# Chunked attention and two feed-forward layers: weighted sum and next scores as one stretch, side work at other times

## The chip, the cores and the metric

The kernel runs on one core of a Trainium2 chip. Times are device microseconds (us) of one execution. Three runs of the kernel before took 1117.49, 1117.62 and 1117.96 us; their median, 1117.62 us, is what the changed kernel is compared with. TensorE is called PE here, its weight loads PEld, VectorE DVE, ScalarE ACT, GpSimd POOL and SyncE, which issues nearly all DMAs, SP.

## The reference

Inputs are float32: q, k, v of 4 batches, 8 heads, 768 positions, 64 values a head; 8 memory keys and values a head; five weight matrices.

```
chunk, left_ctx, right_ctx = (32, 16, 8)           # n_mem = 8
for c in range(nc):                                # 24 chunks
    k_full = concat([mem_k, k[l_start:r_end]])     # 8 + up to 56 keys
    scores = q_c @ k_full.T / 8
    a = exp(scores - max); a = a / (sum(a) + 1e-09)
    out[c] = a @ v_full
x = out as 3072 tokens x 512
h = relu(x @ w_in);  x = (h * h) @ w_out           # 512 -> 2048 -> 512
g = x @ w_gate; silu = g / (1 + exp(-g))
y = (silu * (x @ w_val)) @ w_out2                  # 512 -> 1536 -> 512
```

## The kernel before

**Attention in units.** The 3072 queries are 24 units of 128 queries, all 8 heads each. A unit (class `Unit`) loads q, k and v (L522), and then goes through five steps: `scores` (A: 16 small float32 matmuls, 32 in the trace, into one PSUM bank), `weigh` (B: maximum, subtraction, exponential, sum, reciprocal and scaling, on DVE, ACT and in part POOL), `turn` (T: 16 DVE transposes of 32x32 blocks, L617, or for the first units `turn_pe`, four PE transposes, L639), `mix` (M: the weighted sum of v, 16 small float32 matmuls, L668) and `leave` (L: the result is split in a high and a low part). Units 0 to 3 come first of all, 4 to 7 beside the first quarter of the first feed-forward layer (j = 0), 8 to 23 beside j = 1, 2, 3. The table `BESIDE` says at which step i of which j each letter of a unit is put into the program.

**Feed-forward layers.** All other matmuls work on pairs of fp32r parts, three products for one (`TERMS`). In the first layer four blocks of 512 tokens are done directly: `first_layer` (L843, 12 matmuls) and `first_out` (L870, four times 3 matmuls). For the last two blocks and for the whole second layer, a 2x2 block product is done in seven products: `quads` (L1099) and `out_layer` (L1236). These need sums and differences of weight blocks, the "left sides" (`sides`, `Left`): loaded from DRAM, added on DVE or POOL, split (L467 on ACT, L474 on DVE or POOL), written back to DRAM and loaded again as the weights of the products. The second layer's 18 sides come from the weights in DRAM (`words`), the 16 of the first layer from the parts that j = 1 and 2 wrote back (`whole_of`, L1040). Sums of the data, the "right sides" (`rights`), are made the same way, L486 and L474.

**What sets the order.** The code only lists operations with their buffers and a cost per engine. `Plan.run` then plays them through in its own time and writes the instructions of every engine in the order found. PE takes its operations in listed order, and may take one of the next eight that is ready. The others take the ready operation with the lowest rank; where an operation may go to DVE or POOL, the costs decide (`DIFF`, the `costs` in `split`, `quarter` in `sides`), and `SLOWED` lengthens a DVE operation that runs beside POOL. `SIDES` holds (first due time, spacing, how many) of the left sides. Each engine then works its list strictly in order, so an instruction that waits holds up all behind it.

**Buffers.** PSUM has 8 banks. Pool `A4` has four buffers: one holds the transposed weights of a unit (`pbd`), three its q, k, v. So q and k of the next unit are loaded when `scores` has read the last ones, its v when `mix` has.

**Names in the rows.** In the trace `a` is a buffer of `A4`, `f`, `ff`, `gg` are the side work's, `u` those of the blocks and right sides, `t` small ones of 512, `r`, `rp`, `x`, `xx` hold high and low parts, `ps` is PSUM, `tma`, `tmb`, `tla`, `tlb` are the sides in DRAM.

Of the kernel before, what the change touches and what calls it, by code (L numbers as in the profile page):

```python
# [18 lines left out]
B, H, S, D = 4, 8, 768, 64  # L19
# [7 lines left out]
NF1, NF2 = DFF1 // P, DFF2 // P  # L27
# [34 lines left out]

DUE = 12.0

SLOWED, AVOID = 0.55, 0.3

HOT = ("PS", "T2")

# [17 lines left out]
class Plan:  # L86
# [77 lines left out]
    def run(self, pools, slack=12.0, ahead=8, phases=(), gives=None):  # L164
# [10 lines left out]
        after = {}  # L175
# [36 lines left out]
        def place(o, e):  # L212
            nonlocal moved
            for b in o.bufs:
                if b.pool is not None and b.slot is None:
                    b.slot = free[b.pool].pop(0)
                    queue[b.pool].remove(b)
            o.eng, o.start = e, t
            cost = o.engs[e]
            if e == "DVE" and o.shared:  # L220
                cost += SLOWED * max(0.0, min(cost, engines["POOL"] - t))
            engines[e] = t + cost
            o.end = engines[e] + o.tail
            if o.move:
                moved = max(moved, t) + o.move
                o.end = max(o.end, moved + LANDS + o.tail)
            order.append(o)
            for x in o.engs:
                if x != "PE" and o in ready[x]:
                    ready[x].remove(o)  # L230
            heapq.heappush(events, (o.end, o.n))
            heapq.heappush(events, (engines[e], -1))
# [70 lines left out]

STAGED = 14.5
FIRST = -9.0
SIDES = ((150.0, 22.0, NF2 + NF2 // 2), (560.0, 16.0, NF1))

BY_PE = tuple(range(8))

DIRECT = NB - 2  # L310
C512 = {"ACT": 0.63}
EITHER = {"ACT": 0.63, "DVE": 0.72}
DIFF = {"DVE": 0.69, "POOL": 1.3}
FROM = {"DVE": 0.69}


# [5 lines left out]
def tile_chunked_attention_two_ffn(ctx: ExitStack, tc, qd, kd, vd, w1, w2, wo2, out):  # L322
    nc = tc.nc
    pl = Plan()
# [137 lines left out]
    def split(dst, src, reads, keys, n=512, diff=None):  # L462

        k = n / 512
        pl.op(
            {"ACT": 0.2 + 0.43 * k},
            lambda: nc.scalar.activation(out=dst(HI), in_=src(), func=AF.Copy),  # L467
            reads, [(b, (q, HI)) for b, q in keys],
        )
        costs = {"DVE": 0.16 + 0.56 * k, "POOL": 0.25 + 1.1 * k} if diff is None else diff  # L470

        def low(e):
            eng = nc.gpsimd if e == "POOL" else nc.vector
            eng.tensor_tensor(out=dst(LO), in0=src(), in1=dst(HI).bitcast(F32), op=ALU.subtract)  # L474

        pl.op(
            costs, low, list(reads) + [(b, (q, HI)) for b, q in keys], [(b, (q, LO)) for b, q in keys],
            shared=diff is not FROM,
        )
# [38 lines left out]
    class Unit:  # L518
# [7 lines left out]
                    (), (b,), move=rate(524288),  # L526
                )

        def scores(self):
            u, sc = self.u, pl.buf("PS", "sc")  # L530
            self.sc = sc

            def run():
                q = at(self.q).rearrange("p (s m c q) -> p s m c q", s=2, m=2, c=4)
                k = at(self.k).rearrange("p (s m c k) -> p s m c k", s=2, m=2, c=4)
                o = at(sc).rearrange("p (s f m k) -> p s f m k", s=2, f=2, m=2)
                for p in range(4):
                    s, m = p // 2, p % 2
                    for ci in range(4):
                        f, par = ci // 2, ci % 2  # L540
                        nc.tensor.matmul(  # L541
                            o[64 * par : 64 * par + 64, s, f, m, :], q[:, s, m, ci, :],
                            k[:, s, m, ci, :], start=True, stop=True,
                        )

            pl.op({"PE": 1.16}, run, (self.q, self.k), (sc,), tail=0.2)

            def edge(r, f, a, b):
                o = at(sc).rearrange("p (s f m k) -> p s f m k", s=2, f=2, m=2)
                nc.vector.memset(o[r : r + 64, :, f, :, a:b], NEG)  # L550

            if u % UPB == 0:
                pl.op({"DVE": 0.11}, lambda: edge(0, 0, NMEM, NMEM + LEFT), (), (sc,))
            if u % UPB == UPB - 1:
                pl.op({"DVE": 0.11}, lambda: edge(64, 1, WIN - RIGHT, WIN), (), (sc,))
# [99 lines left out]
                    lambda e, m=m: spread(e, m), (tp,), [(pbd, 4 * m + n) for n in range(4)]  # L655
                )

        def mix(self):
            v, pbd, x = self.v, self.pbd, pl.buf("PS", "x")
            self.x = x  # L660

            def run():
                a = at(v).rearrange("p (h s c d) -> p h s c d", h=2, s=2, c=4)
                b, o = pbd_of(pbd), at(x).rearrange("p (k t) -> p k t", k=4)
                for s in range(2):
                    for ci in range(4):
                        for hh in range(2):
                            nc.tensor.matmul(  # L668
                                o[64 * hh : 64 * hh + 64, 2 * s : 2 * s + 2, CH * ci : CH * ci + CH],
                                a[:, hh, s, ci, :], b[:, hh, s, ci].rearrange("p m q -> p (m q)"),  # L670
                                start=True, stop=True,
                            )

            pl.op({"PE": 1.16}, run, (v, pbd), (x,), tail=0.2)

        def leave(self, xb, a):
            x = self.x
# [21 lines left out]
    def unit(u, pool="A4"):  # L699
        return Unit(u, pool, pool == "S0")  # L700
# [194 lines left out]
    def sides(x, y, store, given=False):  # L895
# [23 lines left out]
        for b in (ax, ay):  # L919
            if 1 not in b.parts:  # L920
                b.parts[1] = [b.parts[0][0], list(b.parts[0][1])]
        quarter = {"DVE": 0.45, "POOL": 0.75}
        POOLED = None
        if not given:
            part(0, ax, 0, reads=((ax, 0), (ax, 1)))
# [394 lines left out]
    for n, x in enumerate(first):  # L1320
# [9 lines left out]
    pairs += [(("out", NF1 - 2), ("out", NF1 - 1))]  # L1330

    units, todo = {}, {}
    BESIDE = (
        (range(4, 8), (2, 5, 8, 11), {"B": 0, "T": 2, "M": 4, "L": 4}),
        ((8, 9, 10, 11, 16, 17), (0, 3, 5, 8, 10, 12), {"B": 1, "T": 2, "M": 3, "L": 3}),
        ((12, 13, 14, 15, 18, 19), (0, 3, 5, 8, 10, 12), {"B": 1, "T": 2, "M": 3, "L": 3}),
        (range(20, 24), (0, 3, 5, 8), {"B": 1, "T": 2, "M": 3, "L": 3}),
    )
    for j, (us, z, d) in enumerate(BESIDE):
        for u, n in zip(us, z):  # L1340
            for op, k in dict(d, A=0).items():
                todo.setdefault((j, n + k), []).append((op, u))

    pend, accs = [], {}

# [8 lines left out]
    for j in range(DIRECT):  # L1354
        if j + 1 < DIRECT:
            xs[j + 1] = pl.buf(("X", "X1")[j % 2], "x")
        for i in range(NF1):
            if j == 0:
                prep1(pairs[i], i == 0)
            for what in "MTLAB":  # L1360
                for op, u in todo.get((j, i), ()):
                    if op != what:
                        continue
                    if op == "A":
                        units[u] = unit(u)
                        units[u].scores()
                    elif op == "B":
                        units[u].weigh()
                    elif op == "T":
                        units[u].turn_pe() if u in BY_PE else units[u].turn()  # L1370
                    elif op == "M":
                        units[u].mix()
                    elif op == "L":
                        if u // 4 < DIRECT:
                            units[u].leave(xs[u // 4], u % 4)
                        else:
                            units[u].leave_far(u // 4 - DIRECT, u % 4)
# [141 lines left out]
```

## Time and profile before

| | |
|---|---|
| median of three runs | 1117.62 us (1117.49 to 1117.96) |
| the profiled execution's own time, and its span | 1114.71 us, 1113.0 us |
| busy: PE, DVE, ACT, POOL | 1087.8, 862.6, 594.7, 199.6 us |
| granted TensorE clock, mean | 0.998 |
| mean DMA rate | 278 GB/s |

The span is the time from the first to the last instruction; the execution has 1.7 us more around it. The profiled execution is 2.9 us shorter than the median of the timed runs, so a difference is carried from one to the other, not a time. Busy PE time is the union of the matmuls' durations; matmuls overlap, so it says when PE has work, not how fast it does it. In the chain that ended last, each piece begins where the one before it ended, so the lengths of its pieces are what the work costs on the path.

Three stretches matter below: the directly done first layer with the attention units beside it (about 65 to 432 us of the span), the passage from the second layer's first quads to their out layer (about 540 to 557), and the second quads with the passage after them (about 612 to 743).

### The profile page before, as it was taken

To read this page: it belongs to the slowest core of one execution; us is meant where nothing else is said; L and a number is where in the kernel's file an instruction comes from. 1 tells how busy PE (TensorE), PEld (TensorE's weight loads), DVE (VectorE), ACT (ScalarE), POOL (GpSimd) and SP (SyncE) were. 2 spreads that over 40 slices of the span, in tenths; PEclk is the share of its full clock that TensorE was granted. 3 is DMA by queue.
4 is the path that set the end of the run, shared out by engine and by line. 5 is a ranking of instruction groups with operands and counts; after the bars stand their busy time and mean duration, and the time that the engine had idled before them with its cause. 6 is when DMAs were issued, how large, how long until landed. Compare 5 with 4: busy or idle time off the path is not lost.

```text
span 1113.0 us, 17104 instructions
## 1 busy us (share of the span) xinstructions
PE 1087.8 (98%) x6044; PEld 892.1 (80%) x6044; DVE 862.6 (77%) x1482; ACT 594.7 (53%) x1007; POOL 199.6 (18%) x165
## 2 busy tenths in 40 slices
PE   5999999999999999999899999999999999999998
PEld 4778888888888887888688888878888887888886
DVE  6999888869979998578999667899747864534971
ACT  4888553555547576456554444564437633433650
POOL 2232101322113343001621100332301000000000
PEclk9999999999999999999999999999999999999999
DMA  9953498888888888999789999989964578655552
GB/s 365 408 228 96 134 311 274 273 289 310 311 289 287 294 290 297 408 341 355 255 298 329 399 405 347 356 315 323 374 222 164 181 240 302 226 189 183 186 171 99
DMA packets 133670, 309.43 MB, mean 278 GB/s; under 512 B 13136, under 2 KB 50000, under 8 KB 133584
## 3 DMA queue, kind: packets, MB, share of 16 engines
q1 hardware_dynamic: 133584, 308.33, 78.6%
q8 instruction: 48, 0.79, 0.3%
q14 instruction: 38, 0.31, 0.1%
HBM read 227.02 MB, written 81.26 MB: 277 GB/s over the span
## 4 chain that ended last, share of the span: by engine, by line
PE 88%; DMA 6%; DVE 4%; issue 1%; ACT 1%; SPq 0%; ACTq 0%
PE ps L1099 36%; PE ps L1236 21%; PE ps L843 14%; PE ps L870 13%; PE ps L668 2%; PE ps L541 2%; DMA a<-yd 1%; DMA rp1float<-in_w 1%; DMA s<-in_k 1%; DMA rp4float<-in_w 1%; DMA rp8float<-in_w 1%; DMA w12float<-in_w 1%; DMA f<-in_w 0%; DMA rp2float32r<-tmb 0%; DVE f L474 0%
## 5 line engine op out<-in xcount | busy, mean ns | idle before, releaser
L495 ACT ACTIVATE t<-ps 128x512 f32<-128x512 f32 x169 | 100.4, 597 | 215.1 <-PE ps L1099 108.6
L486 DVE TENSOR_TENSOR t<-t,ps 128x512 f32<-128x512 f32 x72 | 49.3, 685 | 43.7 <-PE ps L1099 42.6
L474 POOL TENSOR_TENSOR r<-t,r 128x512 fp32r<-128x512 f32 x29 | 45.3, 1562 | 197.9 <-ACT r L467 194.6
L617 DVE STREAM_TRANSPOSE a<-t 32x128 f32<-32x128 f32 x256 | 77.4, 302 | 4.2
L495 ACT ACTIVATE t<-t 128x512 f32<-128x512 f32 x72 | 45.6, 633 | 59.9 <-DVE t L486 59.0
L467 ACT ACTIVATE f<-f 128x512 fp32r<-128x512 f32 (+1 forms) x61 | 33.5, 553 | 30.4 <-DVE f L486 12.5
L486 DVE TENSOR_TENSOR u<-ps,t 128x512 f32<-128x512 f32 x32 | 22.1, 690 | 34.4 <-PE ps L1099 34.3
L486 DVE TENSOR_TENSOR u<-u,u 128x512 f32<-128x512 f32 x61 | 42.5, 712 | 0.1
L486 POOL TENSOR_TENSOR u<-u,u 128x512 f32<-128x512 f32 x12 | 18.8, 1572 | 116.7 <-DVE rp4float32r L474 61.8
L857 ACT ACTIVATE t<-t 128x512 f32<-128x512 f32 x58 | 36.6, 631 | 1.3
L467 ACT ACTIVATE r<-t 128x512 fp32r<-128x512 f32 x54 | 34.1, 631 | 2.8 <-PE ps L870 0.8
L495 ACT ACTIVATE u<-ps 128x512 f32<-128x512 f32 x43 | 25.6, 596 | 17.4 <-PE ps L1099 16.9
L474 DVE TENSOR_TENSOR f<-f,f 128x512 fp32r<-128x512 f32 (+1 forms) x46 | 32.2, 701 | 1.0 <-ACT f L467 0.5
L474 DVE TENSOR_TENSOR r<-t,r 128x512 fp32r<-128x512 f32 x25 | 19.3, 774 | 14.1 <-ACT r L467 14.0
L474 POOL TENSOR_TENSOR x<-u,x 128x512 fp32r<-128x512 f32 x2 | 3.5, 1759 | 135.0 <-ACT x L467 135.0
L486 DVE TENSOR_TENSOR u<-ps,u 128x512 f32<-128x512 f32 x31 | 21.4, 689 | 8.0 <-PE ps L1099 7.7
L580 ACT ACTIVATE t<-t 128x512 f32<-128x512 f32 x24 | 15.1, 629 | 23.3 <-DVE t L573 23.3
L668 PEld LDWEIGHTS ps<-a,a 128*64 128x64 f32 x640 | 20.4, 138 | 6.7 <-issue 3.2
L541 PEld LDWEIGHTS ps<-a,a 128*64 128x64 f32 x640 | 20.4, 138 | 5.3 <-issue 3.2
L668 PE MATMUL ps<-a,a 128*64 128x64 f32 x640 | 23.1, 225 | 0.0
L541 PE MATMUL ps<-a,a 128*64 128x64 f32 x640 | 22.9, 224 | 0.0
L474 POOL TENSOR_TENSOR f<-f,f 128x256 fp32r<-128x256 f32 (+1 forms) x15 | 16.8, 1121 | 34.1 <-DMA f<-wout 25.2
(835 smaller groups left out, 3161.6 us busy)
## 6 DMA issues: line engine op xcount, KB each, us to landing
tma<-f SPq DMA_DIRECT2D x33, 512.0 KB, 4.7
f<-in_w SPq DMA_DIRECT2D x21, 512.0 KB, 6.0
r<-tma SPq DMA_DIRECT2D x21, 512.0 KB, 6.6
a<-in_q SPq DMA_DIRECT2D x20, 512.0 KB, 5.1
a<-in_k SPq DMA_DIRECT2D x20, 512.0 KB, 5.3
a<-in_v SPq DMA_DIRECT2D x20, 512.0 KB, 5.2
x<-tma SPq DMA_DIRECT2D x17, 512.0 KB, 5.8
tmb<-f SPq DMA_DIRECT2D x25, 256.0 KB, 5.5
```

Source lines behind the costliest of these rows:

```text
L467: lambda: nc.scalar.activation(out=dst(HI), in_=src(), func=AF.Copy),
L474: eng.tensor_tensor(out=dst(LO), in0=src(), in1=dst(HI).bitcast(F32), op=ALU.subtract)
L486: eng.tensor_tensor(out=out[1](), in0=x[1](), in1=y[1](), op=op)
L495: nc.scalar.activation(out=out[1](), in_=x[1](), func=func)
L541: nc.tensor.matmul(o[64 * par : 64 * par + 64, s, f, m, :], q[:, s, m, ci, :], k[:, s, m, ci, :], start=True, stop=True,)
L617: nc.vector.transpose(out=o[g : g + 32, hh, :, :, m, :].rearrange("k s (f c) q -> k s f c q", c=2)[:, :, :, par, :], in_=a[r : r + 32, :, ...
L668: nc.tensor.matmul(o[64 * hh : 64 * hh + 64, 2 * s : 2 * s + 2, CH * ci : CH * ci + CH], a[:, hh, s, ci, :], b[:, hh, s, ci].rearrange("p ...
L843: nc.tensor.matmul(at(hp), w1of("in", i, a)[:, k * P : k * P + P], x[:, b, k, :], start=(n == 0), stop=(n == len(terms) - 1),)
L857: nc.scalar.activation(out=at(h), in_=at(h), func=AF.Square)
L870: nc.tensor.matmul(at(accs[m]), w1of("out", i, a)[:, m * P : m * P + P], at(h2)[:, 512 * b : 512 * b + 512], start=(i == 0 and n == 0), st ...
L1099: nc.tensor.matmul(at(bank), at(w[slot])[:, o : o + P], at(r[i, n])[:, 512 * b : 512 * b + 512], start=(first and n == 0 and m == 0), stop ...
L1236: nc.tensor.matmul(at(bank[i][n]), at(w[i][g // 2])[:, o : o + P], at(r)[:, 512 * b : 512 * b + 512], start=(first and m == 0), stop=(g == ...
```

## The change

1. A unit's `mix` and the next unit's `scores` become one operation of PE, in this order, for units 8 to 23; its cost in the plan is 2.2 (1.16 each before). So 15 of the 16 weighted sums stand directly ahead of scores. The steps at which the letters stand come from a list, `SCORES`, and no longer from `BESIDE`.
2. In the plan POOL's costs rise (`DIFF` 1.3 to 1.55, `split` 0.25 + 1.1k to 0.28 + 1.27k, `quarter` 0.75 to 1.1), DVE's fall a little, and the extra time of a DVE operation beside POOL is computed from what POOL has left.
3. `SIDES`: the second layer's 18 sides are spaced by 21 instead of 22. The first layer's 16, before due from 560 on every 16, are due 11 from 612 on every 9 and 5 from 790 on every 12.

```diff
-SLOWED, AVOID = 0.55, 0.3
+SLOWED, AVOID = 0.5, 0.3
...
-                cost += SLOWED * max(0.0, min(cost, engines["POOL"] - t))
+                cost += max(0.0, min(cost, SLOWED * (engines["POOL"] - t)))
...
-SIDES = ((150.0, 22.0, NF2 + NF2 // 2), (560.0, 16.0, NF1))
+SIDES = ((150.0, 21.0, NF2 + NF2 // 2), (612.0, 9.0, 11), (790.0, 12.0, 5))
...
-DIFF = {"DVE": 0.69, "POOL": 1.3}
+DIFF = {"DVE": 0.69, "POOL": 1.55}
...
-        costs = {"DVE": 0.16 + 0.56 * k, "POOL": 0.25 + 1.1 * k} if diff is None else diff
+        costs = {"DVE": 0.16 + 0.53 * k, "POOL": 0.28 + 1.27 * k} if diff is None else diff
...
-        def scores(self):
+        def scores(self, after=None):
             u, sc = self.u, pl.buf("PS", "sc")
             self.sc = sc
+            mixing, reads, writes = after.mixing() if after else (None, (), ())
 
             def run():
+                if mixing:
+                    mixing()
...
-            pl.op({"PE": 1.16}, run, (self.q, self.k), (sc,), tail=0.2)
+            pl.op(
+                {"PE": 2.2 if after else 1.16}, run, (self.q, self.k, *reads), (sc, *writes), tail=0.2
+            )
...
-        quarter = {"DVE": 0.45, "POOL": 0.75}
+        quarter = {"DVE": 0.43, "POOL": 1.1}
...
-    BESIDE = (
-        (range(4, 8), (2, 5, 8, 11), {"B": 0, "T": 2, "M": 4, "L": 4}),
-        ((8, 9, 10, 11, 16, 17), (0, 3, 5, 8, 10, 12), {"B": 1, "T": 2, "M": 3, "L": 3}),
...
+    for u, n in zip(range(4, 8), (2, 5, 8, 11)):
+        for what, k in dict(A=0, B=0, T=2, M=4, L=4).items():
+            todo.setdefault((0, n + k), []).append((what, u))
+    TURNS = (*range(8, 12), 16, 17, *range(12, 16), 18, 19, *range(20, 24))
+    SCORES = (16, 19, 21, 24, 26, 28, 31, 34, 36, 39, 42, 44, 47, 50, 53, 56)
+    for n, (u, g) in enumerate(zip(TURNS, SCORES)):
+        after = SCORES[n + 1] if n + 1 < len(SCORES) else g + 3
+        for what, k in (("A", g), ("B", g + 1), ("T", after - 1), ("L", after)):
+            todo.setdefault(divmod(k, NF1), []).append((what, u))
...
                     if op == "A":
+                        n = TURNS.index(u) if u in TURNS else 0
                         units[u] = unit(u)
-                        units[u].scores()
+                        units[u].scores(units[TURNS[n - 1]] if n else None)
```

**PE, directly done first layer.** Before, in j = 2: L668 is a weighted sum, L541 scores, L843 and L870 the feed-forward layer.

```order
L668 MATMUL ps_91<-a_67,a_70 64x2x32 x16
L843 MATMUL ps_89<-x_66,w10float32r 128x512 x12
L870 MATMUL ps_88<-r_64,w10float32r 128x512 x3
L870 MATMUL ps_93<-r_64,w10float32r 128x512 x3
L870 MATMUL ps_94<-r_64,w10float32r 128x512 x3
L870 MATMUL ps_95<-r_64,w10float32r 128x512 x3
L541 MATMUL ps_90<-a_69,a_68 64x64 x16
```

After, the same layer (L673 is the weighted sum, L544 scores, L852 and L879 the feed-forward layer):

```order
L673 MATMUL ps_91<-a_67,a_68 64x2x32 x16
L544 MATMUL ps_89<-a_70,a_69 64x64 x16
L879 MATMUL ps_94<-r_65,rp0float32r 128x512 x3
L879 MATMUL ps_88<-r_65,rp0float32r 128x512 x3
L879 MATMUL ps_92<-r_65,rp0float32r 128x512 x3
L852 MATMUL ps_95<-xx,rp1float32r 128x512 x12
```

The float32 work of two units now stands together. After the start, a weighted sum and scores stand side by side 16 times, 6 times before; alone between fp32r matmuls stand 7 of them (28 before), and one block of scores now has a PE transpose beside it. From each merged stretch to the next there are 51 to 96 fp32r matmuls, in order 60, 60, 60, 57, 63, 75, 51, 72, 54, 63, 72, 69, 72 and 96, and 75 from the last to the last weighted sum; before there were 72 to 96 from the scores of such a unit to its weighted sum. The loads of the next q, k and v stand behind each merged stretch in SP's list; the latest k stands 18 matmuls ahead of the stretch that needs it.

**DVE, behind the merged stretch that has the fewest matmuls (51) up to the next.** After (L573 to L603 are `weigh`, L622 the transposes; `r`, `f` and `x` in L474 belong to other work):

```order
L573 TENSOR_REDUCE m0_82<-ps1_89 128x8
L474 TENSOR_TENSOR r1_64<-t4_81,r1_64 128x512
L474 TENSOR_TENSOR f2_73<-f3_74,f2_73 128x2x256
L578 TENSOR_TENSOR t0_77<-ps1_89,m0_82 128x512
L474 TENSOR_TENSOR x0_66<-ps3_91,x0_66 128x4x128
L589 TENSOR_REDUCE m2_84<-t0_77 128x8
L594 TENSOR_SCALAR m2_84<-m2_84 128x8
L599 RECIPROCAL m2_84<-m2_84 128x8
L603 TENSOR_TENSOR t0_77<-t0_77,m2_84 128x512
L622 STREAM_TRANSPOSE a0_67<-t0_77 32x4x32 x16
```

Three instructions of other work stand between the unit's own.

**DVE, passage from the second layer's first quads to their out layer.** Before, the last 12 instructions up to the first half of the last quad's bank reads (`f`, `gg` are a left side's):

```order
L486 TENSOR_TENSOR f4_75<-ff2_3230,f4_75 128x256
L486 TENSOR_TENSOR u18_4237<-u18_4237,t3_80 128x512
L486 TENSOR_TENSOR f4_75<-f4_75 128x256
L474 TENSOR_TENSOR gg1_3233<-f3_74,gg1_3233 128x2x256
L474 TENSOR_TENSOR rp9float32r_267<-u5_4224,rp9float32r_267 128x512
L486 TENSOR_TENSOR u21_4240<-ps5_93,t1_78 128x512
L474 TENSOR_TENSOR f2_73<-f4_75,f2_73 128x2x256
L474 TENSOR_TENSOR rp4float32r_688<-u9_4228,rp4float32r_688 128x512
L474 TENSOR_TENSOR rp9float32r_267<-u13_4232,rp9float32r_267 128x512
L486 TENSOR_TENSOR t0_77<-t0_77,ps2_90 128x512
L474 TENSOR_TENSOR rp6float32r_757<-u17_4236,rp6float32r_757 128x512
L486 TENSOR_TENSOR t2_79<-t2_79,ps6_94 128x512
```

After, the same place:

```order
L474 TENSOR_TENSOR f2_73<-f5_76,f2_73 128x2x256
L486 TENSOR_TENSOR a3_70<-a3_70,t1_78 128x512
L486 TENSOR_TENSOR a2_69<-ps6_94,t2_79 128x512
L474 TENSOR_TENSOR f0_71<-f3_74,f0_71 128x2x256
L474 TENSOR_TENSOR rp0float32r_508<-u11_4134,rp0float32r_508 128x512
L486 TENSOR_TENSOR t3_80<-t3_80,ps5_93 128x512
L474 TENSOR_TENSOR rp7float32r_810<-u15_4138,rp7float32r_810 128x512
L486 TENSOR_TENSOR t0_77<-t0_77,ps3_91 128x512
L474 TENSOR_TENSOR rp9float32r_267<-u19_4142,rp9float32r_267 128x512
L486 TENSOR_TENSOR a2_69<-ps2_90,a2_69 128x512
L486 TENSOR_TENSOR u23_4146<-u20_4143,u23_4146 128x512
L486 TENSOR_TENSOR a2_69<-a2_69,t4_81 128x512
```

The last side of the second layer ends at about the same distance from the passage, but with fewer instructions in between, and none of the first layer's follows it: from the last bank read of these quads to that of the out layer, DVE had 21 instructions of sides and now has none. In the same way 62 were 93 in the second quads, 18 are now 6 in the out layer behind them, and 6 are now 34 in the first layer's quads (`first_quads`). In the program's list POOL had 9 instructions in the last 51 matmuls of the first quads; it now has 2 there, and then none for 123 matmuls. Over the whole program POOL has 110 rows (169 before), DVE 1317 (1260). In the second half of the second quads (267 matmuls) SP's DMAs carry 22.3 MB, 20.4 before; in the half ahead of it 20.4, 22.8 before.

## Rows read from the trace of the kernel before

**Rows 1.** Page, busy time, share of span, instructions of each engine.
```profile
PE 1087.8 (98%) x6044; PEld 892.1 (80%) x6044; DVE 862.6 (77%) x1482; ACT 594.7 (53%) x1007; POOL 199.6 (18%) x165
```

**Rows 2.** Waits of PE: who waited for whom, us, times, longest.
```profile
PE ps L541 <- DMA s<-in_k: 9.3, 3, 8.1
PE ps L1099 <- DVE u L486: 3.6, 2, 2.7
...
PE ps L1236 <- ACT f L495: 0.9, 1, 0.9
...
PE ps L1099 <- DVE a L486: 0.7, 1, 0.7
```

**Rows 3.** Chain that ended last, first layer: start, length, what, matmuls.
```profile
102.62 1.08 PE ps L668 x32
103.71 2.95 PE ps L843 x12
106.65 2.72 PE ps L870 x12
...
145.12 1.08 PE ps L668 x32
147.13 2.94 PE ps L843 x12
150.08 2.72 PE ps L870 x12
```

**Rows 4.** Busy by stretch: us, PE, PEld, DVE, ACT, POOL, clock, DMA share, GB/s.
```profile
65.00:402.00 337.00, 337.00 (x2526) 274.85 (x2524) 296.66 (x605) 196.26 (x323) 82.61 (x69) 1.00 0.75 255
...
540.00:557.00 17.00, 13.37 (x57) 10.21 (x56) 17.00 (x22) 11.04 (x21) 9.77 (x7) 1.00 0.82 299
...
619.00:717.00 98.00, 98.00 (x434) 81.19 (x433) 69.34 (x121) 43.73 (x80) 8.58 (x9) 1.00 1.02 374
717.00:743.00 26.00, 24.61 (x108) 19.71 (x106) 25.08 (x36) 14.78 (x28) 12.40 (x10) 1.00 0.93 339
```

**Rows 5.** DVE in order of time: start, us, line, operation, tiles.
```profile
529.70 0.68 DVE L486 TENSOR_TENSOR u<-ps,u 128x512 f32<-128x512 f32 x1
...
531.13 1.78 DVE L486 TENSOR_TENSOR u<-u,t 128x512 f32<-128x512 f32 x1
...
545.23 1.78 DVE L474 TENSOR_TENSOR gg<-f,gg 128x512 fp32r<-128x512 f32 x1
...
558.74 1.89 DVE L486 TENSOR_TENSOR u<-u,u 128x512 f32<-128x512 f32 x3
```

**Rows 6.** POOL in order of time.
```profile
529.19 1.74 POOL L474 TENSOR_TENSOR rp1float32r<-u,rp1float32r 128x512 fp32r<-128x512 f32 x1
531.00 3.05 POOL L486 TENSOR_TENSOR u<-u,u 128x512 f32<-128x512 f32 x2
```

**Rows 7.** PE in order of time, the passage; in brackets idle time before.
```profile
541.98 0.96 PE L1099 MATMUL ps<-rp3float32r,rp9float32r 128*128 128x512 f32 x3 [0.93 <-DVE u L486]
...
554.67 0.96 PE L1099 MATMUL ps<-rp3float32r,x 128*128 128x512 f32 x3 [2.70 <-DVE u L486]
```

**Rows 8.** Groups by form, 65 to 402 us: busy, mean ns, idle before.
```profile
L617 DVE STREAM_TRANSPOSE a<-t 32x128 f32<-32x128 f32 x256 | 77.4, 302 | 4.2
...
L573 DVE TENSOR_TENSOR t<-ps,m 128x512 f32<-128x512 f32 x19 | 13.0, 686 | 0.3
...
L594 DVE RECIPROCAL m<-m 128x8 f32<-128x8 f32 x19 | 3.8, 202 | 1.2
```

**Rows 9.** Groups by form, POOL, 65 to 402 us.
```profile
L474 POOL TENSOR_TENSOR r<-t,r 128x512 fp32r<-128x512 f32 x26 | 40.6, 1563 | 177.4 <-ACT r L467 174.1 <-issue 2.5 <-POOL f L486 0.7
```

**Rows 10.** Page, costliest groups: the exponential.
```profile
L580 ACT ACTIVATE t<-t 128x512 f32<-128x512 f32 x24 | 15.1, 629 | 23.3 <-DVE t L573 23.3
```

**Rows 11.** Page, DMA issues: KB each, median us to landing.
```profile
a<-in_k SPq DMA_DIRECT2D x20, 512.0 KB, 5.3
```

**Rows 12.** Busy by stretch, the second quads: columns as rows 4.
```profile
640.00:670.00 30.00, 30.00 (x134) 24.82 (x134) 19.46 (x36) 12.83 (x24) 2.71 (x3) 1.00 1.04 402
```

More of the change, by code (lines that the diff above doesn't have):

```diff
@@ L656, in turn_pe, with mixing @@
                 )
-        def mix(self):
+        def mixing(self):
             v, pbd, x = self.v, self.pbd, pl.buf("PS", "x")
@@ L672, in run, with mix @@
                             )
-            pl.op({"PE": 1.16}, run, (v, pbd), (x,), tail=0.2)
+            return run, (v, pbd), (x,)
+        def mix(self):
+            run, reads, writes = self.mixing()
+            pl.op({"PE": 1.16}, run, reads, writes, tail=0.2)
         def leave(self, xb, a):
@@ L1332, in tile_chunked_attention_two_ffn @@
     units, todo = {}, {}
-    BESIDE = (
-        (range(4, 8), (2, 5, 8, 11), {"B": 0, "T": 2, "M": 4, "L": 4}),
-        ((8, 9, 10, 11, 16, 17), (0, 3, 5, 8, 10, 12), {"B": 1, "T": 2, "M": 3, "L": 3}),
[L1336 to L1342, printed above, removed]
+    for u, n in zip(range(4, 8), (2, 5, 8, 11)):
[7 more added lines that the diff above has]
+            todo.setdefault(divmod(k, NF1), []).append((what, u))
+        if n + 1 == len(SCORES):
+            todo.setdefault(divmod(after, NF1), []).append(("M", u))
     pend, accs = [], {}
@@ L1359, in tile_chunked_attention_two_ffn @@
                 prep1(pairs[i], i == 0)
-            for what in "MTLAB":
+            for what in "MALBT" if j else "MTLAB":
                 for op, u in todo.get((j, i), ()):
```

## The prediction, made before the changed kernel ran

> **What bounds the kernel now.** I read the page first: PE is busy 1087.8 of 1113.0 us and DVE 862.6 [rows 1], so what a change is worth is PE work taken off, or one of the few holes in PE closed. Then the waits of PE [rows 2]: 9.3 us belong to the first loads, which the change leaves alone; after that the large ones are 3.6 us behind DVE before a bank of the quads (L1099), 0.9 behind ACT in an out layer (L1236) and 0.7 behind DVE, 5.2 us together. Third the chain, which has every piece at its cost on the path [rows 3]: 12 fp32r matmuls take 2.72 us, 0.227 each, but 2.95 when they come right behind float32 work. Last the stretches [rows 4]: beside the attention units PE is busy for 337.00 of 337.00 us with DVE at 296.66; in the passage from 540 to 557 DVE is busy for all of 17.00 us and PE for 13.37; in the second quads PE has no hole and the DMA share is 1.02.
>
> So there are two places where time can go: the PE time of float32 stretches, and 5.2 us of waits, nearly all where DVE is full.
>
> **The merged stretches.** A weighted sum alone takes the path from 102.62 to 106.65, less the 2.72 that the 12 matmuls cost anyhow: 1.31 us. A weighted sum with scores behind it, which the plan of before reached by chance, takes from 145.12 to 150.08, less 2.72: 2.24 us [rows 3]. Two alone are 2.62, so a pair saves 0.38 us: one return to fp32r (0.23), and 0.15 where the second block overlaps the first. There are 16 pairs for 6, so 10 more: 3.8 us. The scores that now have a PE transpose beside them save a return at most, 0.2. Together **-4.0 us**; this is PE work in a stretch without holes, so nothing else hides it. Bounds: 2.3 us if only the returns go (10 x 0.23), 4.1 if all does.
>
> **What the merge makes wait.** The merged operation needs the last unit's transposed weights and the next unit's q and k, and behind it all matmuls of PE queue. The unit's own chain is four 512-wide passes at 0.69, an exponential of 0.63, two small ones at about 0.2 and sixteen transposes at 0.302: 8.6 us [rows 8, 10]. Over 51 matmuls it has 51 x 0.227 + 0.2 = 11.8 us, over 60 it has 13.8, over 72 16.5. In the tightest place DVE carries three other instructions of 512, 2.1 us: 10.7, and some hand-overs between engines. Where POOL runs beside them each can lose 1.1 (below). The next k stands 18 matmuls, 4.1 us, ahead of the stretch that needs it in the worst case, and a load lands in 5.3 [rows 11]; SP can issue it earlier than it is listed if nothing holds its queue. From both sides: nothing, if all is as above; and 25 us, if each chain takes the whole 16.3 us (72 x 0.227) that the plan of before left it (the distances fall short of 72 by 111 matmuls in all, x 0.227). The rows lie near the lower end: I take **+0.9 us**, 0.15 at each of the six distances of 60 and less.
>
> **POOL's work to DVE.** 59 rows leave POOL, 57 come to DVE. Three 512-wide passes in a row take 1.89, 0.60 to 0.63 each [rows 5], so DVE gains up to 36 us of work, and POOL loses up to 59 x 1.56 = 92 [rows 9]. DVE gets something back: beside POOL a pass with two tiles in SBUF took 1.78 instead of 0.68 (at 531.13, while POOL ran from 531.00; again at 545.23), though one that reads PSUM took 0.68 at 529.70 beside POOL's 1.74 [rows 5, 6]. So each POOL instruction can cost DVE 1.1, and 59 fewer give back 0 to 65 us: DVE's sum ends between -29 and +36, and I take 0. Only where DVE is full does it count.
>
> The Trainium skill has a rule for these rows (SBUF — State Buffer, "Who interferes with whom"): the port pair that DVE and GpSimd share is an exclusive lock, taken by a DVE instruction with two SBUF inputs, and the later one is blocked until the earlier has ended. The trace agrees: 1.78 is 0.68 behind a rest of POOL's instruction, and the pass with a PSUM input is not touched. By a proportional share of the port the 1.78 would follow from every pass beside POOL, and moving work would give back nothing on average. The sum above does not need the rule.
>
> **The passage from 540 to 557.** The waits are 0.93 and 2.70 us, both for DVE to read a bank [rows 7]. 22 instructions took 17.00 us there [rows 4]; at 0.63 they are 13.9, so 3.1 us or more were lost to POOL and went into the bank reads' delay. After the change POOL has 2 instructions there for 9, and the 21 instructions of sides behind the last quad are gone. What is late next is DVE itself: its passes stand back to back for the out layer's right sides, about as many as PE has time for. Bounds: -3.9 (the waits and 0.12 twice for restarting, 0.96 against 0.84 for three matmuls) and 0 if DVE stays behind. I take **-3.0 us**.
>
> **The passage from 717 to 743.** Waits of 0.7 and 0.9 [rows 2]; DVE is busy for 25.08 of 26.00 us, POOL for 12.40 [rows 4]. Sides there fall from 18 instructions to 6 in the out layer, but the quads before it get 93 for 62 and some of them wait for DMAs in DVE's queue, with the bank reads behind them. Bounds -1.8 and +2; I take **-0.6 us**.
>
> **The second quads and the later ones.** 31 more instructions of sides, up to 20 us of DVE, go into about 107 us where DVE was busy for 70% [rows 4]; the first layer's quads get 28 more, 18 us, where DVE has as much room. Hidden, unless a bank read stands behind a side that waits. DMA: 22.3 MB in 267 matmuls (60.5 us) is 369 GB/s, and 402 was reached over 30 us [rows 12]. So nothing from there; a remainder of **+0.1**.
>
> **Sum.** -4.0 + 0.9 - 3.0 - 0.6 + 0.1 = -6.6 us. The profiled execution took 1114.71 (span 1113.0 and 1.7 around it), so one like it would take 1108.1. It stands 2.9 us under the median of the timed runs, and I carry the difference: 1117.62 - 6.6 = **1111.0 us**, 0.6% faster.
>
> **Rivals.**
>
> *Only the merge pays.* DVE keeps its backlog at the passages, since what POOL gave up is now DVE's own work, and the waits stay or move: -4.0 + 0.4 = -3.6, 1114.0 us. For it: DVE has no room from 540 to 557, and 57 rows more. Against it: seven of those nine POOL instructions are gone.
>
> *The merged stretch is a new wait.* PE queues behind transposes or loads at distances shorter than the 72 matmuls of before. If the chains use half of the 25 us above, 12.6 us come back against 7.6 won (4.0 + 3.0 + 0.6): 1117.62 + 5.0 = 1122.6 us, slower. It decides from 0.5 us for each of the 15 stretches on. For it: DVE is at 88% there and its list is strict [rows 4]; the k that is listed 4.1 us ahead. Against it: 3 us of cover in the tightest place, and PE had no hole from 65 to 402 us before.
>
> *DMA in the second quads.* The sides come every 9 us instead of 16, the share is already 1.02 [rows 4], and the loads of weights come behind them. If the stretch goes no faster than the 374 GB/s of its mean, 22.3 MB take 59.6 us, still within 60.5; at 340 it would be 65.6 and cost 5 us: 1116.1, no change. The Trainium skill (SBUF — State Buffer, table in "A bandwidth-pool intuition that's wrong (but worth ruling out)") gives about 358 GB/s from HBM to a core; by that the stretch takes 62.3 us and costs 1.8, 1112.8 us. The trace had 402 here over 30 us, and the measurement decides.
>
> **How the numbers follow.** The forecast, 1109 to 1112.5: 0.45. Better than that, all waits gone and none new (-8.5): 0.1. Only the merge pays, 1112.5 to 1115.4: 0.24. DMA or smaller waits eat it, within 0.2% (2.2 us, about what a measurement of this kernel tells from no change), 1115.4 to 1119.9: 0.13. New waits at the merged stretches: 0.08. So faster 0.79, same 0.13, slower 0.08. The range leaves out the slow rival and half of the no-change case at the top, and the last tenth of the better one at the bottom: 1107.5 to 1117.
>
> **What would show it.** In the chain of the changed kernel, pairs of 2.0 us with one 2.95 behind them, at 16 places, and PE busy time down by about 4 us: otherwise the first step is wrong. PE's waits after 65 us at about 2.5 us instead of 5.2, the two for DVE at the first passage gone or under 0.7 together, and no DVE pass of 1.78 there. A wait of L673 or L544 for a transpose or for `in_k`, more than 0.5 us on average, would make the second rival right; waits of L1108 for `tma`, the third. POOL's busy time should fall by 60 to 90 us and DVE's sum stay within 35. If PE's waits stay above 5 us, the first rival holds.

## The result, and the profile after

The changed kernel takes 1105.64 us (median of 4 runs, 1103.88 to 1108.38) against 1117.79 us for the one before (4 runs, 1117.49 to 1118.93) on the same chip. The ratio is 0.9895, 95% interval 0.9881 to 0.9909: 12.15 us or 1.05% faster. The forecast was 1111.0 us, with 1107.5 as the lower end, so the direction was right and the gain nearly twice what was forecast. The profiled execution took 1106.09 us with a span of 1104.3, 8.7 us below the span of before.

The page's busy times after, to be held against [rows 1]:

```profile
PE 1082.3 (98%) x6044; PEld 892.0 (81%) x6044; DVE 860.0 (78%) x1540; ACT 594.1 (54%) x1010; POOL 126.5 (11%) x106
```

PE has 5.5 us less to do, POOL 73 us less, and DVE's sum is 2.6 us lower although it took over what POOL gave up. The waits of PE after (who waited for whom: us, times, longest), against [rows 2]:

```profile
PE ps L544 <- DMA s<-in_k: 9.3, 3, 8.1
...
PE ps L1108 <- DVE rp9float32r L474: 0.2, 1, 0.2
PE ps L1108 <- ACT a L495: 0.2, 1, 0.2
```

Only the lines of the quads (L1108) are of the time after 65 us: 0.4 us of waiting are left of 5.8. The chain after (start, length, what, matmuls) shows the merged pair of [rows 3], smaller groups behind other pairs, and the long pieces:

```profile
146.22 1.08 PE ps L673 x32
148.24 2.95 PE ps L852 x12
...
246.68 2.27 PE ps L879 x9
...
260.48 1.58 PE ps L879 x6
...
431.37 112.88 PE ps L1108 x498
...
548.33 46.24 PE ps L1245 x204
...
612.25 103.36 PE ps L1108 x456
...
719.69 44.88 PE ps L1245 x198
```

A pair lasts 2.02 us, then one group is 0.23 us longer than elsewhere: 2.95 for 12 matmuls, 2.27 for 9, 1.58 for 6 (2.72, 2.04 and 1.36 elsewhere). Such a return from float32 work to fp32r stands 36 times in PE's order between 65 and 436 us before, and 25 times after: 11 returns fewer, 2.5 us. The piece from 431.37 is one stretch of matmuls through all first quads, without a hole. Stretches at the places of [rows 4], the last two moved and lengthened (us, PE, PEld, DVE, ACT, POOL, granted clock, DMA share, GB/s):

```profile
65.00:402.00 337.00, 337.00 (x2517) 278.24 (x2516) 290.62 (x609) 195.97 (x323) 58.23 (x52) 1.00 0.73 254
540.00:557.00 17.00, 17.00 (x76) 14.08 (x75) 16.97 (x29) 12.46 (x24) 0.00 (x0) 1.00 0.98 362
615.00:715.00 100.00, 100.00 (x443) 82.77 (x443) 72.80 (x130) 45.30 (x83) 2.99 (x2) 1.00 1.02 381
715.00:750.00 35.00, 35.00 (x156) 29.00 (x155) 33.20 (x59) 23.52 (x43) 3.44 (x2) 1.00 0.96 348
```

In the passage DVE is as full as before, but does 29 instructions in 17 us where it did 22: POOL has none there. DVE in order of time shows its passes back to back; the longest between 540 and 557 us takes 0.69, none the 1.78 us of [rows 5]:

```profile
545.26 0.67 DVE L486 TENSOR_TENSOR u<-u,u 128x512 f32<-128x512 f32 x1
545.86 0.68 DVE L486 TENSOR_TENSOR a<-a,t 128x512 f32<-128x512 f32 x1
546.46 0.68 DVE L474 TENSOR_TENSOR rp4float32r<-a,rp4float32r 128x512 fp32r<-128x512 f32 x1
```

**Where the 8.7 us of span came from.** The chain's fixed points in both traces: the wait of the first layer at 62.27 us stands at 63.58 (+1.3, among the first loads; a second profile of the changed kernel has it at 62.28); from there to the end of the first layer -4.7; from there to the last matmul -5.6; behind it +0.3. So the part that the change touches is 10.3 us shorter. The +1.3 goes with the granted clock (1.00 is TensorE's full 2.4 GHz, 0.50 the lower level of 1.2) among the first loads, here from 28 to 36 us, before and after:

```profile
28.00:36.00 8.00, 7.04 (x23) 5.34 (x24) 7.93 (x11) 5.55 (x8) 0.00 (x0) 0.79 1.02 408
28.00:36.00 8.00, 6.25 (x17) 4.92 (x18) 7.71 (x10) 5.11 (x8) 0.00 (x0) 0.57 1.02 408
```

The second profile of the changed kernel has 0.79 there, and of two more of the kernel before (below) one has 0.79 and the wait at 62.20, the other 0.57 and the wait at 63.81. So this difference belongs to the execution and not to the change.

### The profile page after: what moved, and what is told of

Its sections match the earlier page's. It is cut to its first block, busy times and chain, and to the rows that moved or that the text cites. A ratio compares the mean times of both kernels' runs of the same rounds, so it can differ in the third digit from the quotient of the medians.

```text
span 1104.3 us, 17051 instructions
## 1 busy us (share of the span) xinstructions
PE 1082.3 (98%) x6044; PEld 892.0 (81%) x6044; DVE 860.0 (78%) x1540; ACT 594.1 (54%) x1010; POOL 126.5 (11%) x106
## 4 chain that ended last, share of the span: by engine, by line
PE 95%; DMA 2%; ACT 1%; DVE 1%; issue 0%; SPq 0%; ACTq 0%
PE ps L1108 37%; PE ps L1245 22%; PE ps L852 16%; PE ps L879 15%; PE ps L673 2%; PE ps L544 2%; DMA rp0float<-in_w 1%; DMA s<-in_q 1%; ACT f L765 0%; SPq L525 0%; DVE u L486 0%; PE ps L644 0%; ACT f L772 0%; DVE f L486 0%; DVE rp3float32r L815 0%
## 5 line engine op out<-in xcount | busy, mean ns | idle before, releaser
L622 DVE STREAM_TRANSPOSE a<-t 32x128 f32<-32x128 f32 x256 | 77.4, 303 | 4.3
L486 DVE TENSOR_TENSOR u<-u,u 128x512 f32<-128x512 f32 x70 | 48.2, 711 | 0.1
L474 POOL TENSOR_TENSOR r<-t,r 128x512 fp32r<-128x512 f32 x21 | 29.8, 1420 | 147.8 <-ACT r L467 107.8
L467 ACT ACTIVATE f<-f 128x512 fp32r<-128x512 f32 (+1 forms) x60 | 32.4, 546 | 15.3 <-DVE f L486 10.2
L474 DVE TENSOR_TENSOR f<-f,f 128x512 fp32r<-128x512 f32 (+1 forms) x52 | 32.7, 631 | 9.6 <-ACT f L467 9.2
L474 DVE TENSOR_TENSOR r<-t,r 128x512 fp32r<-128x512 f32 x32 | 22.1, 689 | 22.6 <-ACT r L467 22.5
L486 DVE TENSOR_TENSOR u<-ps,t 128x512 f32<-128x512 f32 x26 | 17.9, 689 | 26.5 <-PE ps L1108 24.9
L585 ACT ACTIVATE t<-t 128x512 f32<-128x512 f32 x24 | 15.1, 630 | 22.3 <-DVE t L578 22.3
L673 PEld LDWEIGHTS ps<-a,a 128*64 128x64 f32 x640 | 20.3, 138 | 6.7 <-issue 4.9
L673 PE MATMUL ps<-a,a 128*64 128x64 f32 x640 | 23.0, 225 | 0.0
L544 PE MATMUL ps<-a,a 128*64 128x64 f32 x640 | 22.3, 223 | 0.0
L802 DVE CUSTOM_DVE_ANT_0 f<-f,f 128x2048 uint16<-128x2048 uint16 (+1 forms) x17 | 22.0, 1294 | 0.3
L544 PEld LDWEIGHTS ps<-a,a 128*64 128x64 f32 x640 | 20.4, 138 | 1.8 <-issue 1.4
L474 POOL TENSOR_TENSOR rp9float32r<-u,rp9float32r 128x512 fp32r<-128x512 f32 x2 | 5.9, 2972 | 127.2 <-ACT rp9float32r L467 115.9
L467 ACT ACTIVATE x<-u 128x512 fp32r<-128x512 f32 x26 | 16.3, 626 | 7.6 <-PE ps L1245 4.2
```

The costliest lines, as they stand in the source:

```text
L486: eng.tensor_tensor(out=out[1](), in0=x[1](), in1=y[1](), op=op)
L544: nc.tensor.matmul(o[64 * par : 64 * par + 64, s, f, m, :], q[:, s, m, ci, :], k[:, s, m, ci, :], start=True, stop=True,)
L622: nc.vector.transpose(out=o[g : g + 32, hh, :, :, m, :].rearrange("k s (f c) q -> k s f c q", c=2)[:, :, :, par, :], in_=a[r : r + 32, :, ...
L673: nc.tensor.matmul(o[64 * hh : 64 * hh + 64, 2 * s : 2 * s + 2, CH * ci : CH * ci + CH], a[:, hh, s, ci, :], b[:, hh, s, ci].rearrange("p ...
```

## The experiments

**The parts, alone and by twos.** Three edits, by their numbers in the list of the change: *merge* (1), *costs* (2) and *due times* (3), put into the kernel before or taken out of the changed one.

*The whole change again.* 

> The changed kernel again, with a second profile, beside the kernel before on this chip. The two profiles so far differ by 8.6 us (1114.71 to 1106.09), the medians by 12.2. Theory 1 (the profile of before was a short run): the ratio stays at 0.989 to 0.991 and the new profile is again near 1106, at the median of its timed runs. Theory 2 (the median of the changed kernel was lucky): the ratio comes out at 0.992 to 0.994. PE's waits after 65 us stay under 1 us by both; the start (first 12 fp32r matmuls of L852 that use rp4 begin at 62.3 before, 63.6 after) varies by a us or two if it is chance, and not if it is the changed order.

*Merge alone.* 

> The kernel before with the merged stretches and the list SCORES alone: costs, SLOWED and SIDES as before. 16 pairs, POOL 174 instructions. Theory 1 (the merge saves PE work and nothing else): 4 to 5 us, ratio 0.9955 to 0.9965, PE's waits after 65 us still 4 to 7 us at the passages. Theory 2 (the merge also moves DVE's work so that the passages open): 8 us or more, ratio under 0.993, waits under 2 us. Rival from the prediction (the merged stretches wait): under 2 us gained, waits of L673 or L544 of more than 2 us.

*Costs alone.* 

> The kernel before with the plan's costs alone (DIFF, split, quarter, SLOWED and its formula): POOL 121 instructions for 170, float32 stretches as before (39 for 39). Theory 1 (POOL's work beside DVE is what keeps DVE behind at the passages): PE's waits after 65 us fall from 5.2 to under 2, 3 to 5 us gained, ratio 0.9955 to 0.9975. Theory 2 (the sides' due times are what counts): no more than 1.5 us, ratio over 0.9985, the waits at 540 to 557 still over 2 us.

*Due times alone.* 

> The kernel before with SIDES alone: POOL 168 instructions, stretches as before. Theory 1 (POOL): the passages still wait, 3 us or more after 65 us, ratio 0.998 to 1.0. Theory 2 (due times): waits under 2 us, 3 to 5 us gained, ratio 0.9955 to 0.9975.

*Merge and costs.* 

> The changed kernel with the old due times of the sides (22 and 16 us), so the merge and POOL's new costs only. Theory A (the parts go together: right costs keep POOL off the passages, right due times keep a side from standing ahead of a bank read): the one wait of about 2.5 us at the first passage that the costs alone left stays, with the merge's 3.7 on top: 1116.4 - 2.4 - 3.7 = 1110.3 us, ratio 0.9945, waits of PE after 65 us about 3. Rival B (the due times do nothing once POOL's costs are right): no wait above 0.7 us and the time of the whole change, 1105 to 1106 us, ratio 0.990.

*Costs and due times.* 

> The kernel before with the new costs and the new due times, without the merge. Theory A: the 13 us of waits that the new due times alone brought came from POOL's underestimated costs; with the right ones there are none above 0.7 us, and what is missing from the whole change is the merge alone: 1105.6 + 4 = 1109.5 us, ratio 0.9938. Rival B (the due times fit only the plan that the merge gives): waits of 8 us and more after 65 us, 1122 us or above.

*Merge and due times.* 

> The changed kernel with POOL's old costs. Theory A: POOL again takes some 165 instructions, and the waits of the due times alone come back, 10 us or more after 65 us; 1131.8 - 3.7 = 1128 us, ratio 1.010. Rival B (the merge makes the new due times harmless): 1108 us or less, waits under 3 us.

Measured, each against the kernel before in the same comparison (1116.39 us for the single edits and all three, 1116.32 for the twos); the waits of PE after 65 us and POOL's busy time are those of the profiled execution:

| edits | median us | ratio, 95% interval | waits us | POOL us |
|---|---|---|---|---|
| merge | 1112.65 | 0.9971 (0.9960 to 0.9982) | 5.9 | |
| costs | 1113.98 | 0.9980 (0.9970 to 0.9990) | 3.0 | 153.5 |
| due times | 1131.84 | 1.0138 (1.0121 to 1.0156) | 13.2 | 201.3 |
| merge, costs | 1113.05 | 0.9967 (0.9953 to 0.9980) | 5.1 | 161.2 |
| costs, due times | 1112.46 | 0.9966 (0.9953 to 0.9979) | 3.9 | 144.9 |
| merge, due times | 1119.06 | 1.0027 (1.0017 to 1.0038) | 11.1 | 199.4 |
| all three | 1105.56 | 0.9907 (0.9894 to 0.9920) | 2.0 | |

The effects do not add: -3.7, -2.4 and +15.4 us alone, -10.8 together. The whole change has the ratio that theory 1 expected, but its second profile has 2.0 us of waits where both theories had less than 1. Merge alone gained a little less than its range says, with the waits that it says. Costs alone fit neither theory: the small waits went, but one of 2.51 us stayed at the first passage. Due times alone were expected to gain or to do nothing; they are the one edit that harms. PE's waits with it, in the kernel before:

```profile
PE ps L1099 <- ACT t L495: 4.8, 3, 3.6
PE ps L1099 <- DVE u L486: 2.8, 1, 2.8
PE ps L668 <- DVE a L617: 2.6, 1, 2.6
PE ps L1099 <- DVE a L486: 2.5, 2, 1.5
```

There are now waits of over 1.5 us at four places (405, 549, 726 and 845 us) instead of one. With the old costs the plan gives POOL some 160 instructions whatever the due times, and ahead of the first three waits the sides' passes on DVE run long beside POOL's. Ahead of the last, POOL has nothing to do; a side's instruction stands in ACT's list and waits for a DMA, and the work that PE needs stands behind it. One row ahead of the wait at 549 from DVE and POOL each, and ACT ahead of that at 845:

```profile
546.82 1.75 DVE L474 TENSOR_TENSOR gg<-f,gg 128x512 fp32r<-128x512 f32 x1
546.58 1.45 POOL L486 TENSOR_TENSOR u<-a,u 128x512 f32<-128x512 f32 x1
843.29 0.63 ACT L467 ACTIVATE gg<-f 128x512 fp32r<-128x512 f32 x1 [6.90 <-DMA tlb<-gg]
```

With the new costs the harm is gone (1112.46), and with all three 2.0 us are left, nearly all in one wait. The expectations hit costs with due times only in sign (1109.5 expected: four waits of 0.6 to 0.9 us were left), merge with costs only in part (1110.3; two waits instead of one), and missed merge with due times (1128 expected): in the merged plan the worst waits are 2.1 us instead of 3.6.

**What a wait costs.** In the profile of `due times` the three waits of more than 2.5 us, and in the second profile of the changed kernel one of 1.77 us, were followed by matmuls at half speed; PE in order of time in the latter, in brackets the idle time ahead:

```profile
927.18 0.50 PE L1108 MATMUL ps<-rp9float32r,rp6float32r 128*128 128x512 f32 x1 [1.77 <-ACT rp9float32r L467]
...
928.70 1.49 PE L1108 MATMUL ps<-x,rp6float32r 128*128 128x512 f32 x3
929.98 1.49 PE L1108 MATMUL ps<-rp9float32r,rp0float32r 128*128 128x512 f32 x3
```

Three matmuls take 0.84 elsewhere. In the profile that the forecast rests on, the 2.70 us wait had no such thing behind it. So a pause of known length was put ahead of every quad of the changed kernel:

```diff
+nc.tensor.matmul(at(bank)[:16, :16], fill, fill, start=True, stop=True)
+for _ in range(n):                      # 2, 5, 9 in turn
+    nc.gpsimd.memset(fill, 0.0)
+nc.tensor.matmul(at(bank)[:16, :16], fill, fill, start=True, stop=True)
```

> The changed kernel with a pause put into PE's queue ahead of every quad of both FFNs: a small matmul, then 2, 5 or 9 small memsets on POOL that wait for it, then a small matmul that waits for the last of them, so that PE stands still for three known lengths in turn. Theory C (a wait also costs granted clock behind it, in some executions and not in others): the windows behind the longer pauses show a granted clock of 0.6 to 0.8 in some places and 1.00 in others, the time rises by more than the sum of the pauses, and the runs spread by several us with the mean granted clock, the slower ones at the lower. Rival D (the clock falls by itself, whatever the waits, or only the start differs): granted clock 1.00 behind all pauses, and the time rises by the sum of the pauses (and 0.23 us each for the return to fp32r) within 2 us.

Measured 1187.29 us (1182.8 to 1188.53); the mean granted clock of the runs goes from 0.991 in the shortest to 0.986 in the three longest. Two of the pauses of the profiled execution, PE in order of time:

```profile
451.43 0.22 PE L1112 MATMUL ps<-fill 128*16 128x16 f32 x2 [1.63 <-POOL fill L1111]
451.57 1.48 PE L1116 MATMUL ps<-r,rp8float32r 128*128 128x512 f32 x3
452.85 1.48 PE L1116 MATMUL ps<-rp5float32r,rp8float32r 128*128 128x512 f32 x3
454.13 1.36 PE L1116 MATMUL ps<-rp0float32r,r 128*128 128x512 f32 x3
455.33 0.86 PE L1116 MATMUL ps<-rp7float32r,r 128*128 128x512 f32 x3
...
486.48 0.21 PE L1112 MATMUL ps<-fill 128*16 128x16 f32 x2 [1.64 <-POOL fill L1111]
486.62 0.96 PE L1116 MATMUL ps<-r,r 128*128 128x512 f32 x3
487.42 0.85 PE L1116 MATMUL ps<-rp5float32r,r 128*128 128x512 f32 x3
488.11 0.84 PE L1116 MATMUL ps<-rp0float32r,rp8float32r 128*128 128x512 f32 x3
488.79 0.84 PE L1116 MATMUL ps<-rp7float32r,rp8float32r 128*128 128x512 f32 x3
```

The two waits are equal, 1.63 and 1.64 us. Behind the first, nine matmuls take 3.76 us, behind the second 2.17: 1.59 us lost. The granted clock of both stretches (columns as above):

```profile
451.50:454.50 3.00, 3.00 (x9) 2.33 (x10) 0.79 (x2) 0.14 (x1) 0.00 (x0) 0.55 0.62 253
...
486.50:489.50 3.00, 3.00 (x15) 2.47 (x16) 1.67 (x4) 0.60 (x1) 0.00 (x0) 1.00 0.99 306
```

1.00 is the level of 2.4 GHz; 0.55 is nearly all at 1.2. It fell behind 6 of the 14 pauses of some 1.6 us (1.57 to 1.82) and behind none of the 30 of 0.46 to 0.99. Theory C holds, and two more kernels put it to the test, with `n` 2 and 5, and 9 alone:

> The changed kernel with a pause ahead of all 44 quads, of 2 and 5 small memsets in turn (0.46 and 0.96 us of waiting, none of 1.6). Theory C: behind waits below 1 us the clock stays at 1.00, so 44 x (0.71 + 0.52 for the two small matmuls and the restart) = 54 us more, 1160 us, mean granted clock 0.997 to 0.998, and all runs within some 3 us. Rival F (every stop of PE costs clock now and then): granted clock below 0.99 and 1170 us or more.

> The same with 9 memsets in each pause, 44 waits of about 1.64 us. Waits and restarts alone: 44 x (1.64 + 0.52) = 95 us, 1200.6 us. Theory C: with 1.7 us of lost clock behind 6 to 10 of every 14 pauses, as before, 32 to 53 us more, 1233 to 1254 us, granted clock 0.96 to 0.975. Rival D (the waits cost their length alone): 1201 us, granted clock 0.995 or above.

Measured 1161.16 us (1161.07 to 1164.32; clock 0.996 to 1.000) and 1243.71 us (1242.06 to 1244.53; clock 0.961 to 0.964). The waits of the two, short first:

```profile
PE ps L1112 <- POOL fill L1111: 31.3, 44, 1.0
```

```profile
PE ps L1112 <- POOL fill L1111: 72.4, 44, 1.8
```

Waits and the small matmuls (22.9, 44 times the 0.52 of the expectation) explain 1105.6 + 31.3 + 22.9 = 1159.8 us of the short one, but only 1200.9 of the long one. The long one's profile has half-speed matmuls behind 25 of the 44 waits; 25 x 1.59 = 40 us, 1241 in all. The short one's has none; but one of its runs, 1164.32 us at 0.996, lost some 3 us at places that no trace shows. So a wait of 1.6 us costs its length, and 1.6 us more in about half of its occurrences.

Shorter waits are not safe where they stand close together. Among the neighbours of the changed kernel below, `r4_due_600` has waits of 0.52, 0.22 and 0.70 us within 2.7 us, and the clock fell behind them (PE in order of time, then the stretch with its granted clock):

```profile
925.89 0.50 PE L1108 MATMUL ps<-rp6float32r,rp3float32r 128*128 128x512 f32 x1 [0.52 <-ACT rp6float32r L467]
...
928.05 1.95 PE L1108 MATMUL ps<-rp4float32r,rp3float32r 128*128 128x512 f32 x3 [0.70 <-ACT rp4float32r L467]
929.80 1.48 PE L1108 MATMUL ps<-rp6float32r,rp7float32r 128*128 128x512 f32 x3
...
928.00:931.50 3.50, 3.45 (x8) 2.44 (x9) 3.47 (x6) 3.05 (x6) 0.00 (x0) 0.51 1.03 409
```

`r4_no_pool` shows the same at 933 us, behind waits of 0.40, 0.22, 0.73 and 0.22.

**The kernel before, twice more.** Unchanged, for its profile.

> The kernel before again, for a second profile. Theory C (a long wait of PE is followed by about 1.7 us of lost clock in most executions): the wait of about 2.7 us at the first passage is followed by some 3 us at a granted clock of 0.55 to 0.85, against 1.00 in the profile that the forecast was made from, and the time is then 1116 to 1118 us instead of 1114.7. Rival E (the distance from the profile to the median arises at the start, among the first loads): the clock behind that wait is 1.00 and the stretch up to 65 us is longer by 1.5 us or more.

> The kernel before once more, as the run ahead of it: theory C has the clock fall behind the wait of 2.7 us in at least one of these two; rival E in neither.

The first took 1116.55 us. PE behind the wait of [rows 7], in order of time:

```profile
554.33 0.96 PE L1099 MATMUL ps<-rp3float32r,x 128*128 128x512 f32 x3 [2.74 <-DVE u L486]
555.12 1.13 PE L1099 MATMUL ps<-r,x 128*128 128x512 f32 x3
556.05 2.76 PE L1236 MATMUL ps<-rp3float32r,x 128*128 128x512 f32 x6
558.61 1.70 PE L1236 MATMUL ps<-rp9float32r,rp2float32r 128*128 128x512 f32 x6
```

Six matmuls took 1.54 at this place in the profile that the forecast rests on. From the wait's end to the fourth group of L1236 (at 561.51 here, at 560.26 there) it is 7.18 against 5.59 us: 1.59 again. The second took 1118.0 us, with the clock at 1.00 behind the wait: there the wait of 62.27 us stood at 63.81, and a wait of 1.18 us stood at 939 us. So both theories have a share, and the longer start too goes with the clock, 0.57 from 28 to 36 us as shown above; the forecast's profile was an execution in which none of these happened.

**Design or luck?** Since the parts don't add, four neighbours of the changed kernel, each with another plan:

```diff
 r4_due_600
-(612.0, 9.0, 11)
+(600.0, 9.0, 11)
 r4_pool_costs
-"POOL": 1.55}
+"POOL": 1.6}
-"POOL": 0.28 + 1.27 * k
+"POOL": 0.28 + 1.32 * k
 r4_second_due_old
-(612.0, 9.0, 11), (790.0, 12.0, 5)
+(560.0, 16.0, NF1)
 r4_no_pool                     # DIFF, split, quarter
+"POOL": 90
```

> The changed kernel with the second group of due times beginning at 600 instead of 612, which gives another plan (over a thousand rows of PE's order stand elsewhere). Theory M (what counts is that no side is due in the passage from 540 to 557 and that POOL is off it): waits after 65 us below 1.5 us and 1104.5 to 1108 us. Rival L (the plan of the change is a lucky one): waits of 3 us and more, 1109 to 1113 us as for the changes by twos.

> The changed kernel with POOL's costs 0.05 us higher still (1.6 for 1.55 and 1.32 for 1.27 per 512), another plan again. Theory M: 1104.5 to 1108 us, waits below 1.5 us. Rival L: 1109 to 1113 us.

> The changed kernel with its second and third group of due times replaced by the old second one (560 on, every 16 us); the first group stays at 21. Theory M: the three sides due at 560, 576 and 592 come into the passage, so a wait of 1.5 to 3 us stands there again, with its share of lost clock behind it: 1108.5 to 1112 us. Rival (only the first group's 21 instead of 22 cleared the passage): 1105 to 1107 us.

> The changed kernel with POOL priced out of the shared passes, so that POOL keeps 33 instructions of 110 and DVE has 67 more. If a POOL instruction gives DVE as much as it takes (the forecast's step, net 0), DVE's sum stays within 30 us of 860 and the time at 1105 to 1108 us; if DVE misses the help at the passages, its sum rises by 40 us or more, waits of 3 us and more come there, and the time is 1110 us or above; if POOL only costs, the time falls below 1104.5 us.

Measured against 1116.51 us: 1105.87 (ratio 0.9904, 0.9885 to 0.9924), 1109.01 (0.9935, 0.9920 to 0.9949), 1107.99 (0.9925, 0.9908 to 0.9941), 1107.41 us (0.9929, 0.9908 to 0.9949). They keep 7.5 to 10.6 us, at least two thirds of the 10.8 of the second comparison and more than any change by twos: theory M, though `r4_pool_costs` stands 1 us above its range, at the border of theory L, with 2.7 us of waits, one of 1.17 back at the first passage. `r4_second_due_old` is a miss for theory M: no wait came back between 540 and 557 us (the largest is 0.76 at 617). It differs from merge with costs only in the first group's 21 for 22: with 22 waits of 1.27 and 2.30 us stood at the passage, and the time was 1113.05. So this spacing cleared the passage; the other groups are worth some 2 us by the medians, which is not clear of noise. Without POOL's share of the shared passes, the page says:

```profile
PE 1084.7 (98%) x6044; PEld 894.3 (81%) x6044; DVE 862.7 (78%) x1608; ACT 597.5 (54%) x1020; POOL 20.9 (2%) x30
```

POOL has 76 instructions fewer than in the changed kernel; DVE does 68 more and is busy for 2.7 us more: what POOL takes off DVE it gives back in longer passes beside it. There is no wait at either passage here, and 1107.41 us is what the forecast's net of 0 expected. The Trainium skill (SBUF — State Buffer, "Who interferes with whom") calls the port pair that the two share an exclusive lock; these sums fit that, but by themselves don't tell it from a port that slows both. None of the four beats the changed kernel.

## Why the prediction was wrong

The mechanisms were the right ones, and none of the rivals occurred; but the sizes of the waits were off, all to one side, and so the range missed. The step that failed is what the sum did with PE's waits: it let 2.0 us of the waits and restarts at the passages stay, where all of them went, and added 0.9 at the merge, where none came.

- **The merged stretches, -4.0.** Right. 11 returns went, 2.5 us, and in 10 more pairs the second block overlaps the first by 0.15 us, 1.5: 4.0 us by 10 pairs and one more return, as the step counted. The first layer is 4.7 us shorter; 0.32 of it is a wait at 431.95 that is gone, and 0.27 a group behind 68 us that took 2.99 us before and takes 2.72 (3.03 and 3.01 in the other profiles of before, 2.72 in the other one of after). The sum had neither; why that group was slower stays open.
- **What the merge makes wait, +0.9.** Nothing: 337.00 of 337.00 us busy. The working gave 8.6 to 10.7 us for a chain that has 11.8 or more; the 0.15 each was added against it and rests on no row.
- **The passages, -3.0 and -0.6.** Wrong in size. All of it went, 5.2 us of waits and the restarts, -5.6 with two small ones. This was the outer bound of the first (-3.9) and near that of the second (-1.8); I shaded both for DVE staying behind, though the step's own rows had nine POOL instructions falling to two and 3.1 us lost to them. The best case of the forecast has the same fault: "all waits gone and none new" was put at -8.5, but -4.0 with the two outer bounds is -9.7.
- **POOL's work to DVE, 0.** Right: 57 rows moved to DVE, and its sum fell by 2.6; 68 more cost 2.7.
- **The rest, +0.1.** Right for DMA: share 1.02 at 381 GB/s, no wait for `tma`.
- **The sum against the median.** In the traces 10.3 us against the 6.6 forecast: 1107.3 us by that alone, just under the range. In the medians it is 12.15 and, on another chip, 10.8. The weak step here is "I carry the difference": the 2.9 us from the profile to the median are no constant of the program. A part of it hangs on the waits that the change removes: 1.59 us of clock behind the 2.7 us wait in one of three profiles of before, and a longer start and a further wait in another. But the 1.85 us from 10.3 to 12.15 are not clear of noise: the interval of the ratio is 10.2 to 13.3 us, and on the other chip 0.5 is left. In 18 runs of the kernel before on one chip the time goes with the mean granted clock (correlation -0.84, 1114.3 and 1114.86 at 1.000, 1117.88 at 0.995).

The failed steps, by size: the passages (2.0 with the small waits), the carried difference (1.85, 12.15 less 10.3), the waits added at the merge (0.9), and 0.8 in the wait at 431.95, the group behind 68 us and the rest: 5.55, which is 12.15 less 6.6. How the carried 1.85 divides between the clock at the start, the clock behind waits, late waits and noise was not settled: three profiles are too few.

## What to carry to other kernels

A wait of PE can cost more than its length: behind waits of 1.6 us, or behind shorter ones close together, count the clock too, and look for it in several executions before the distance between a profile and a median is carried over. Where a planner's costs and its due times were tuned together, an edit of one alone says little: the same due times cost 15 us with wrong costs and gained 7.5 with right ones beside the merge. And where a chain fits into its distance by the rows, no wait should be added out of caution; that belongs into the range.

## What the runs showed of the hardware

Two waits of the same length (1.63 and 1.64 us), in one execution and ahead of the same work, were followed by a granted clock of 0.55 and of 1.00. Behind waits of 1.57 to 1.82 us it fell 6 of 14 and 25 of 44 times, and where the loss was measured it was 1.59 us. The length of the single wait does not decide it: none of 74 pauses of up to 0.99 us was followed by a fall in a profile, while three waits of 0.52, 0.22 and 0.70 us close together were, and one of 2.70 us was not. What decides it, no run here shows. And POOL's 76 instructions in the shared passes relieve DVE of 2.7 us in all.
